# First stage of an adaLN linear-attention block: products of ones without a reader, products with silu(c) on repeated columns, another order of the first loads

## The chip, the core and the metric

The kernel runs on one core of a Trainium2 chip. The metric is the time of the device in microseconds, the median of several runs. The engines are TensorE (PE; PEld is its weight load), VectorE (DVE), ScalarE (ACT), GpSimd (POOL) and SyncE (SP), which issues most of the DMAs. All data are fp32; "fp32r" is the type in which most products run, with each operand split into a rounded part (hi) and the rest (lo).

## What is computed

`x` is 2048 x 576 (`S` x `D`), `c` is 1 x 576, `w_mod` is 576 x 3456.

```
mod = silu(c) @ w_mod                      # 6 rows of 576: sa, ca, ga, sb, cb, gb
h = layernorm(x) * (1 + ca) + sa
x = x + ga * linear_attention(h, wqkv, wo) # 32 heads of 18
h = layernorm(x) * (1 + cb) + sb
x = x + gb * (silu(h @ w1) @ w2)           # F = 4608
```

## The kernel before

The rows of x are worked on in 16 tiles of 128 rows, four to a block. Before any product of the attention can run, the kernel needs the first piece of `mod` (`sa` and `ca`) as columns, because it modulates the normalised, transposed x: chunk k of 128 features (five chunks, k = 0 to 4, the last with 64) gets `h = xT * scale + shift`, with scale and shift from `cols["a"]`, in the traces `col_a`.

The first stage, up to the products of the first two tiles with the weights of the keys, is written out by hand under `tc.manual_schedule()` (L374 to L454). Its order:

- `ident`, `ones`, `sel` and small constants are set; c is loaded as a row (`crow`), transposed on PE (L387) and turned into `sc = silu(c)`, one column per 128 features.
- Four tiles of x are loaded first (L259), then the pieces of `w_mod` of 128 rows and 2 x 576 columns into `mods[0]` to `mods[3]` (L265 to L269, `load_mod`), with the last 64 rows in `tmod` on ACT's queue, then `wqkv` in 15 pieces into the accumulators `acc` (keys, values, queries).
- `ln.stats`, `ln.finish` and `ln.normalise` are the layernorm of the four tiles: `bn_stats` on DVE, a power on POOL (L170), and the normalisation on DVE or ACT (L177, L179).
- The modulation is split. `mods[0]` and `mods[1]` go straight to PE (`mod_direct`, `mod_mm`, L329): the weights of the product are 128 columns of `w_mod`, the moving operand is one column of `sc`. `tmod` goes the same way with two columns, `sel`. `mods[2]` and `mods[3]` are scaled by `sc` and added on DVE (L340, L409) and their sum goes to PE with one column of `ones` (`col_mod`). All of these add up in PSUM, chunks 0 and 1 (`HEAD`) in one place, chunks 2 to 4 in another, so `col_a` is read in two steps (L348).
- `turn_tiles` transposes tiles 0 and 1 (L354). Chunk by chunk, `modulate` (L185, L187) and `split_h` (L191, L109) make hi and lo of h, `w_hi` (L282, on ACT) and `w_lo` (L287, L289, on POOL or DVE) make hi and lo of the weights, and `first_k` multiplies (`k_part`, L371). A second pass over the lo parts of the weights follows, one tile after the other.
- `k_phi` (L298 on ACT, `e`; L303 and L304 on DVE) applies phi to the keys.

What comes after, the values, tiles 2 and 3 (`turn_half`), the queries and the other blocks, is ordered on PE by the program and on the other engines by a planner with an estimate of times; a later part follows the lists in `ORDERS`.

Of the kernel before, what the change touches and what calls it, by code (L numbers as in the profile page):

```python
# [9 lines left out]
F32 = mybir.dt.float32  # L10
# [6 lines left out]
P = 128  # L17
# [5 lines left out]
def kernel(ctx: ExitStack, tc, A_x, A_wqkv, A_wo, B_x, B_w1, B_w2, c, w_mod, out):  # L23
# [28 lines left out]
    def f32(ap):  # L52
        return ap.bitcast(F32)
# [183 lines left out]
    def psT():  # L237
        t = psA.tile([P, 512], F32, name="psT")
        return t
# [16 lines left out]
    nc.scalar.dma_start(crow[0:KC, :], c[0, 0 : KC * P].rearrange("(j p) -> j p", p=P))  # L256
    nc.scalar.dma_start(crow[KC : KC + 1, :].rearrange("p (h r) -> p h r", h=2),
                        c[0:1, KC * P : D].unsqueeze(1).to_broadcast([1, 2, 64]))
    xts = x0s = [load_x(0, i) for i in range(4)]  # L259


    mod_room = hTa.tile([P, KC, 2, DX], F32, name="hT")
# [18 lines left out]
    def w_hi(wpart, k, full):  # L281
        return A.copy(wpart(k if k < KC else 2 * KC), full)  # L282
# [42 lines left out]
    def mod_mm(m, k, rhs, a=None, first=False, last=False):  # L325

        c = 2 * (k - HEAD if k >= HEAD else k)
        dst = mod_ps_a[k >= HEAD][:, c : c + 2] if a is None else mod_ps_a[k >= HEAD][:, c + a : c + a + 1]
        T.matmul(dst, m[:, k * P : (k + 1) * P], rhs, start=first, stop=last, skip_group_check=True)  # L329

    def mod_direct(m, rhs, first=False):
        A.copy(m[:, :, D:DX], m[:, :, KC * P : D])
# [4 lines left out]
    def add_mod(k0, k1):  # L337

        o = sums[:, :, k0 * P : min(k1 * P, D)]
        V.scalar_tensor_tensor(o, mods[3][:, :, k0 * P : min(k1 * P, D)], sc[:, 3:4], o, op0=ALU.mult, op1=ALU.add)  # L340
        if k1 > KC:
            V.tensor_copy(sums[:, :, D:DX], sums[:, :, KC * P : D])

    def col_mod(k0, k1):
        for k in range(k0, k1):
            for a in range(2):
                mod_mm(sums[:, a], k, ones[:, 0:1], a, last=True)
        V.tensor_add(cols["a"][:, k0:k1, :], mod_ps_a[k0 >= HEAD].rearrange("p (k a) -> p k a", a=2),  # L348
                     plus1.unsqueeze(1).to_broadcast([P, k1 - k0, 2]))

    def turn_tiles(pT, tiles, chunks):
# [15 lines left out]
    def k_part(tiles, passes, first=False, last=False):  # L367
        for n, (a, b) in enumerate(passes):
            for i in tiles:
                for h in range(2):  # L370
                    T.matmul(kps[i][:, h, :HALF], hT[0][:, a, i * P : i * P + P], wk_(b)[:, h * HALF : (h + 1) * HALF],  # L371
                             start=first and n == 0, stop=last and n == len(passes) - 1)

    with tc.manual_schedule():  # L374
        make_identity(nc, ident)
        V.memset(ones, 1.0)
        V.memset(sel, 0.0)
        V.memset(neghalf, -0.5)
        V.memset(eps, EPS)
# [7 lines left out]
        T.transpose(psc, crow, ident[: KC + 1, : KC + 1])  # L387
# [16 lines left out]
        pT = dict(enumerate((t[:, 0:256], t[:, 256:512], kvp[1][:, 0, :], kvp[1][:, 1, :], kvp[2][:, 0, :])))  # L404
# [8 lines left out]
        def first_k(k):  # L413
            k_part(range(2), [(k, k), (KC + k, k)], k == 0)
# [1065 lines left out]
```

## Time and profile before

| | |
|---|---|
| median of three runs | 1168.71 us (1167.72 to 1171.38) |
| span of the profiled execution | 1167.7 us; no other time of this execution is told |
| busy: PE, DVE, ACT, POOL | 1144.4, 977.4, 531.2, 660.1 us |
| first product with a piece of `w_mod` | 10.25 us |
| first and second `col_a` | 24.39 and 30.39 us |
| `e` of tile 0 (ACT L298) | 37.65 us |
| first product with `wq` | after 52.74 us |

The times in the table's lower half are from the timeline and from the chain of waits. In the profile, L12 is line 12 of the kernel. A row of the timeline has the start, the duration, the engine, the line, the operation, the tiles (out<-in), the shape, the count, and the idle time of the engine before it with what ended it. A product of fp32 (not fp32r) stands as two records of PE.

### The profile page before, as it was taken

Reading aid. Unit: us, or ns where it says so; the run is one execution under the profiler, and the core shown is the slowest. Engines: PE = TensorE matmul, PEld = TensorE weight load, DVE = VectorE, ACT = ScalarE, POOL = GpSimd, SP = SyncE. Lnnn points to the kernel's source line nnn. Section 1 sums busy time; section 2 is a strip of 40 time slices with the busy share of each in tenths; the row PEclk is TensorE's granted clock in tenths of the full one; section 3 lists DMA queues with packets and bytes.
Section 4 is the critical chain, followed back from the end, with each engine's and each line's share of the span. In section 5 each row is a group of like instructions: output and inputs, shape, how many; then the busy total and the mean of one; then the engine's idle time right before and its main releaser. Section 6 shows DMA issues by size and latency. Waiting matters only on the chain.

```text
span 1167.7 us, 19567 instructions
## 1 busy us (share of the span) xinstructions
PE 1144.4 (98%) x7203; PEld 1058.8 (91%) x7203; DVE 977.4 (84%) x1539; ACT 531.2 (45%) x1088; POOL 660.1 (57%) x749
## 2 busy tenths in 40 slices
PE   6899999999999999999999999999999999999998
PEld 6799999999998889999999999999999999999998
DVE  3857574478797899999999999999999999999996
ACT  3553433346556454444444454444444444444541
POOL 2500000164554387677677767757767776776686
PEclk9999999999999999999999999999999999999999
DMA  8303210022357879769769779688697697697684
GB/s 284 102 28 105 64 55 1 1 83 63 112 218 266 322 261 348 274 254 351 272 252 363 266 280 334 262 319 308 249 352 275 257 345 273 255 364 268 256 308 152
DMA packets 57231, 268.61 MB, mean 230 GB/s; under 512 B 5484, under 2 KB 19312, under 8 KB 34096
## 3 DMA queue, kind: packets, MB, share of 16 engines
q1 hardware_dynamic: 56964, 267.06, 62.2%
q8 instruction: 57, 0.93, 0.3%
q10 hardware_dynamic: 172, 0.30, 0.1%
q14 instruction: 38, 0.31, 0.1%
HBM read 250.56 MB, written 16.78 MB: 229 GB/s over the span
## 4 chain that ended last, share of the span: by engine, by line
PE 94%; DVE 2%; DMA 2%; ACT 1%; issue 0%; SPq 0%; DVEq 0%; ACTq 0%
PE up L1211 33%; PE down L1284 31%; PE psK L212 12%; PE big L212 7%; PE small L774 2%; PE big L785 2%; PE kvp L517 1%; PE kvp L329 1%; PE psK L668 1%; PE big L700 1%; DMA room<-hd 1%; DVE hT L109 1%; PE small L200 1%; DMA hT<-in_w_mod_dram 1%; PE up L1314 1%; PE down L1314 1%
## 5 line engine op out<-in xcount | busy, mean ns | idle before, releaser
L1292 DVE TENSOR_TENSOR acc<-down,acc 128x576 f32<-128x576 f32 x330 | 246.2, 754 | 14.1 <-PE down L1284 4.3
L1211 PE MATMUL up<-hT,w 128*128 128x512 f32 x916 | 240.3, 391 | 0.0
L1211 PEld LDWEIGHTS up<-hT,w 128*128 128x128 f32 x916 | 164.6, 188 | 25.8
L1246 POOL TENSOR_TENSOR s<-f,f 128x256 f32<-128x256 f32 x66 | 51.6, 782 | 163.9 <-ACT f L1227 163.9
L1284 PE MATMUL down<-w,hc 128*128 128x288 f32 x792 | 120.7, 294 | 0.0
L1284 PE MATMUL down<-w,hb 128*128 128x288 f32 x792 | 120.7, 294 | 0.0
L1284 PEld LDWEIGHTS down<-w,hb 128*128 128x128 f32 x792 | 113.5, 188 | 6.0 <-DVE U L1292 0.4
L1284 PEld LDWEIGHTS down<-w,hc 128*128 128x128 f32 x792 | 113.6, 188 | 5.6
L1292 DVE TENSOR_TENSOR U<-down,U 128x576 f32<-128x576 f32 x132 | 99.5, 754 | 18.0 <-PE down L1284 15.7
L109 DVE TENSOR_TENSOR w<-v,w 128x288 fp32r<-128x288 f32 (+1 forms) x170 | 111.8, 667 | 0.4 <-ACT w L954 0.4
L212 PE MATMUL psK<-w,hT 128*128 128x288 f32 (+2 forms) x660 | 108.0, 298 | 0.8 <-DVE w L287 0.6
L212 PEld LDWEIGHTS psK<-w,hT 128*128 128x128 f32 x660 | 95.0, 189 | 1.5 <-DVE w L287 0.8
L1211 PE MATMUL up<-room,w 128*128 128x512 f32 x348 | 93.2, 396 | 1.7 <-DMA room<-hd 1.7
L1265 POOL TENSOR_TENSOR hc<-s,hc 128x512 fp32r<-128x512 f32 x66 | 89.8, 1360 | 0.0
L1227 ACT ACTIVATE f<-f 128x512 f32<-128x512 f32 x102 | 64.4, 631 | 48.1 <-DVE f L1232 25.7
L1230 DVE TENSOR_TENSOR f<-up,p 128x512 f32<-128x512 f32 x102 | 69.7, 683 | 14.7 <-PE up L1211 10.1
L1211 PEld LDWEIGHTS up<-room,w 128*128 128x128 f32 x348 | 62.4, 188 | 13.0 <-DVE f L1232 2.1
L954 ACT CAST w<-v 128x288 fp32r<-128x288 f32 x85 | 36.5, 434 | 77.0 <-PE down L1284 52.1
L1250 POOL TENSOR_TENSOR f<-f,s 128x256 f32<-128x256 f32 x66 | 50.6, 767 | 34.4 <-DVE hb L1265 27.3
L1284 PE MATMUL down<-w,hd 128*128 128x288 f32 x396 | 63.2, 295 | 0.0
L1284 PE MATMUL down<-w,he 128*128 128x288 f32 x396 | 63.1, 295 | 0.0
L1284 PE MATMUL down<-w,ha 128*128 128x288 f32 x396 | 63.0, 294 | 0.0
(284 smaller groups left out, 2498.4 us busy)
## 6 DMA issues: line engine op xcount, KB each, us to landing
hT<-hd SPq DMA_DIRECT2D x66, 1280.0 KB, 5.8
hT<-hd SPq DMA_DIRECT2D x45, 1024.0 KB, 5.1
room<-hd SPq DMA_DIRECT2D x35, 1280.0 KB, 6.0
room<-hd SPq DMA_DIRECT2D x20, 1024.0 KB, 5.8
v<-in_B_w_dram SPq DMA_DIRECT2D x17, 576.0 KB, 7.3
v<-in_B_w_dram SPq DMA_DIRECT2D x17, 512.0 KB, 7.6
hd<-S SPq DMA_DIRECT2D x6, 1024.0 KB, 4.2
xt<-in_A_x_dram SPq DMA_DIRECT2D x16, 288.0 KB, 3.1
```

Source lines behind the costliest of these rows:

```text
L109: return V.tensor_sub(lo, full, f32(hi))
L212: T.matmul(ps, xpart(a), wpart(b), start=n == 0, stop=n == len(XW) - 1)
L774: T.matmul(ps, left, right, start=n == 0, stop=n == len(seq) - 1)
L954: A.copy(self.w2[n][:, 0], src)
L1211: T.matmul(ps, left, right, start=first and m == 0, stop=m == len(seq) - 1, skip_group_check=True)
L1227: A.activation(self.f[i, k], self.f[i, k], AF.Silu)
L1230: V.tensor_add(f, self.bank[bank[1]], self.p1)
L1246: G.tensor_add(self.s[:, 0:1], half(i, 0, 1), half(i, 1, 1))
L1250: G.tensor_sub(half(i, 1, 0), half(i, 1, 0), self.s[:, 1:2])
L1265: eng.tensor_sub(t[:, :, 1, :], src, f32(t[:, :, 0, :]))
L1284: T.matmul(ps[:, p, :HALF], self.a[i, n][:, u, p * P : (p + 1) * P], self.w.w2[n][:, v], start=n in (1, 5, 7, 6) and j == 0, stop=j == 2, ...
L1292: V.tensor_add(dst, ps[:, :, :HALF], dst)
```

## The change

Three things change, all in the first stage.

*Loads.* Tiles 2 and 3 of x are loaded behind the four pieces of `w_mod` instead of ahead of them. Their statistics, with a second `ln.finish`, move behind the sums of the modulation (tile 2) and the split of chunk 1 (tile 3), and their normalisation, on ACT, behind the casts of the key weights.

*Products with silu(c).* The moving operands get more columns: `scw` is 128 equal columns of `sc` (128 are used for chunks 0 and 1, 80 for chunks 2 to 4), `sel` is 48 columns twice, `ones` is used with 128 or 80 columns. The results lie in slots of 128 or 80 columns of two PSUM banks, of which one column is read. `scw` and `sel` are made on DVE in `z`, which is free until later; `mods[1]`'s products come ahead of the tail's and the transposes; the fifth transposed chunk gets another bank, and a copy of 64 columns moves from DVE to ACT.

*Products of ones.* `warm_up(8)` and `warm_up(10)` multiply `ones` with `ones` (128 columns) around the transpose of c; nothing reads the result.

```diff
-    xts = x0s = [load_x(0, i) for i in range(4)]
+    xts = x0s = [load_x(0, i) for i in range(2)]
...
     for k in range(1, KC):
         load_mod(mods[k], 0, k)
+    xts += [load_x(0, i) for i in range(2, 4)]
...
-    sel = pa.tile([P, 2], F32, name="sel")
+    WIDE, SLOTS = 48, (P, 80)
+    scw = z[:, : 2 * P].rearrange("p (j w) -> p j w", j=2)
+    sel = z[:, 2 * P : 2 * P + 2 * WIDE].rearrange("p (a w) -> p a w", a=2)
...
-    mod_ps_a = kvp[0][:, 0, 0 : 2 * HEAD], kvp[2][:, 1, 0 : 2 * (KC + 1 - HEAD)]
+    mod_bank = [kvp[j].rearrange("p a b -> p (a b)") for j in (0, 2)]
+    mod_slots = [b[:, : n * w].rearrange("p (k a w) -> p k a w", a=2, w=w)
+                 for b, n, w in zip(mod_bank, (2 * HEAD, 2 * (KC + 1 - HEAD)), SLOTS)]
+
+    def mod_mm(m, k, rhs, a, first=False, last=False):
+
+        slots, k0 = mod_slots[k >= HEAD], HEAD if k >= HEAD else 0
+        w = SLOTS[k >= HEAD]
+        dst = slots[:, k - k0, :, 0:WIDE] if a is None else slots[:, k - k0, a, :]
+        T.matmul(dst, m[:, k * P : (k + 1) * P], rhs if a is None else rhs[:, 0:w], start=first, stop=last, skip_group_check=True)
...
         if k1 > KC:
-            V.tensor_copy(sums[:, :, D:DX], sums[:, :, KC * P : D])
+            A.copy(sums[:, :, D:DX], sums[:, :, KC * P : D])
...
+    warm_ps = ps2()
+
+    def warm_up(n):
+        for _ in range(n):
+            T.matmul(warm_ps[:, 0, 0:P], ones, ones, start=True, stop=True)
...
+        warm_up(8)
         psc = psT()[:, : KC + 1]
         T.transpose(psc, crow, ident[: KC + 1, : KC + 1])
+        warm_up(10)
         A.activation(sc, psc, AF.Silu)
         A.activation(warm, sc[:, 0:1], AF.Exp)
         ln.stats(0, xts[0])
+        for j in range(2):
+            V.tensor_scalar(scw[:, j, :], ones, sc[:, j : j + 1], None, op0=ALU.mult)
         for a in range(2):
-            A.copy(sel[a * 64 : a * 64 + 64, a : a + 1], sc[a * 64 : a * 64 + 64, KC : KC + 1])
-        for i in range(1, 4):
-            ln.stats(i, xts[i])
-        ln.finish()
+            rows = slice(a * 64, a * 64 + 64)
+            V.tensor_scalar(sel[rows, a, :], ones[rows, 0:WIDE], sc[rows, KC : KC + 1], None, op0=ALU.mult)
+        ln.stats(1, xts[1])
+        ln.finish(0, 2)
 
-        mod_direct(mods[0], sc[:, 0:1], True)
+        mod_direct(mods[0], scw[:, 0, :], True)
         A.copy(tmod[:, D:DX], tmod[:, KC * P : D])
-        for k in START:
-            mod_mm(tmod, k, sel)
         ln.normalise(0, xts[0], xts[0], V)
         ln.normalise(1, xts[1], xts[1], A)
+        mod_direct(mods[1], scw[:, 1, :])
+        for k in START:
+            mod_mm(tmod, k, sel, None)
...
-        mod_direct(mods[1], sc[:, 1:2])
-        for i in (2, 3):
-            ln.normalise(i, xts[i], xts[i], A)
...
         add_mod(HEAD, KC + 1)
+        ln.stats(2, xts[2])
         first_k(0)
         col_mod(HEAD, KC + 1)
         turn_tiles(pT, (0, 1), (KC,))
         w_hi(wk_, 1, acc[1])
         split_h(*args[1])
+        ln.stats(3, xts[3])
+        ln.finish(2, 4)
         first_k(1)
...
         w_hi(wk_, 4, acc[4])
+        for i in (2, 3):
+            ln.normalise(i, xts[i], xts[i], A)
```

More of the change, by code (lines that the diff above doesn't have):

```diff
@@ L322 @@
     HEAD = 2
-    mod_ps_a = kvp[0][:, 0, 0 : 2 * HEAD], kvp[2][:, 1, 0 : 2 * (KC + 1 - HEAD)]
[L325 to L329, printed above, removed]
+    mod_bank = [kvp[j].rearrange("p a b -> p (a b)") for j in (0, 2)]
[6 more added lines that the diff above has]
+        T.matmul(dst, m[:, k * P : (k + 1) * P], rhs if a is None else rhs[:, 0:w], start=first, stop=last, skip_group_check=True)
     def mod_direct(m, rhs, first=False):
@@ L346, in col_mod @@
             for a in range(2):
-                mod_mm(sums[:, a], k, ones[:, 0:1], a, last=True)
-        V.tensor_add(cols["a"][:, k0:k1, :], mod_ps_a[k0 >= HEAD].rearrange("p (k a) -> p k a", a=2),
+                mod_mm(sums[:, a], k, ones, a, last=True)
+        V.tensor_add(cols["a"][:, k0:k1, :], mod_slots[k0 >= HEAD][:, :, :, 0],
                      plus1.unsqueeze(1).to_broadcast([P, k1 - k0, 2]))
@@ L372, in k_part @@
                              start=first and n == 0, stop=last and n == len(passes) - 1)
+    warm_ps = ps2()
+    def warm_up(n):
+        for _ in range(n):
+            T.matmul(warm_ps[:, 0, 0:P], ones, ones, start=True, stop=True)
     with tc.manual_schedule():
+        V.memset(ones, 1.0)
         make_identity(nc, ident)
-        V.memset(ones, 1.0)
         V.memset(sel, 0.0)
@@ L390 @@
         ln.stats(0, xts[0])
+        for j in range(2):
+            V.tensor_scalar(scw[:, j, :], ones, sc[:, j : j + 1], None, op0=ALU.mult)
         for a in range(2):
-            A.copy(sel[a * 64 : a * 64 + 64, a : a + 1], sc[a * 64 : a * 64 + 64, KC : KC + 1])
-        for i in range(1, 4):
-            ln.stats(i, xts[i])
-        ln.finish()
-        mod_direct(mods[0], sc[:, 0:1], True)
+            rows = slice(a * 64, a * 64 + 64)
[3 more added lines that the diff above has]
+        mod_direct(mods[0], scw[:, 0, :], True)
         A.copy(tmod[:, D:DX], tmod[:, KC * P : D])
-        for k in START:
-            mod_mm(tmod, k, sel)
         ln.normalise(0, xts[0], xts[0], V)
         ln.normalise(1, xts[1], xts[1], A)
+        mod_direct(mods[1], scw[:, 1, :])
+        for k in START:
+            mod_mm(tmod, k, sel, None)
         t = psT()
-        pT = dict(enumerate((t[:, 0:256], t[:, 256:512], kvp[1][:, 0, :], kvp[1][:, 1, :], kvp[2][:, 0, :])))
+        pT = dict(enumerate((t[:, 0:256], t[:, 256:512], kvp[1][:, 0, :], kvp[1][:, 1, :], kvp[0][:, 0, :])))
         turn_tiles(pT, (0, 1), range(KC))
-        mod_direct(mods[1], sc[:, 1:2])
-        for i in (2, 3):
-            ln.normalise(i, xts[i], xts[i], A)
         V.tensor_scalar(sums[:, :, 0:D], sums[:, :, 0:D], sc[:, 2:3], None, op0=ALU.mult)
```

## The prediction

> **What bounds the kernel now.** I read the page first, then the chain of waits up to 90 us, because the diff touches nothing later than that; then the timelines of the engines in that stretch.
>
> ```profile
> span 1167.7 us, 19567 instructions
> PE 94%; DVE 2%; DMA 2%; ACT 1%; issue 0%; SPq 0%; DVEq 0%; ACTq 0%
> ...
> 10.25 6.53 PE kvp L329 x30
> ...
> 18.59 5.78 PE kvp L329 x28
> ...
> 24.39 0.17 DVE col_a L348
> ...
> 28.77 1.59 PE kvp L329 x12
> 30.39 0.17 DVE col_a L348
> ...
> 37.65 0.66 ACT e L298
> ...
> 52.74 0.39 PE kvp L517
> 53.13 12.71 PE psK L212 x84
> ```
>
> The whole span is TensorE's, 94% of the chain. So what the first stage takes is added to a long run of products that waits for nothing, and an early gain is kept one for one if everything after it keeps its order. In the built programs it does: behind the first stage all five engines have the same instructions in the same order before and after.
>
> The chain to 24.39 us is almost only L329, the modulation's products. From 30.39 on it passes between DVE, ACT and POOL until the first product with `wq`, just after 52.74; from there it is PE again.
>
> Why are the L329 products slow? They have one column each, and two records per product (20 records for the ten products of a piece). The rows below are of the timeline, of single lines (least, median and longest ns), and of the table by stretches: its columns are the stretch, its length, the busy time and records of PE, PEld, DVE, ACT and POOL, the granted clock, the DMA share and GB/s. The last row is a group of the stretch 25.97 to 29.38.
>
> ```profile
> 22.51 1.84 PE L329 MATMUL kvp<-ones,hT 128*128 128x1 f32 x8
> L329 PE MATMUL kvp<-ones,hT x20: 205/352/353, 22.5 to 30.1; 128*128 128x1 f32 x20
> 115.72 1.06 PE L475 MATMUL psK<-ones,tmod 128*128 128x128 f32 x8
> L475 PE MATMUL psK<-ones,tmod x20: 274/275/377, 115.5 to 153.4; 128*128 128x128 f32 x20
> 114.15 1.21 PE L482 MATMUL psK<-tmod,ones 128*128 128x288 f32 x4 [0.17 <-DVE vx L109]
> 19.14:22.55 3.41, 3.41 (x18) 3.41 (x18) 0.00 (x0) 0.00 (x0) 0.00 (x0) 1.00 1.05 335
> 25.97:29.38 3.41, 3.41 (x17) 3.40 (x16) 2.17 (x3) 0.94 (x3) 1.42 (x1) 1.00 0.40 97
> 29.38:32.79 3.41, 3.04 (x23) 2.73 (x23) 1.66 (x5) 2.17 (x5) 0.55 (x1) 1.00 0.23 78
> 49.86:53.27 3.41, 1.34 (x9) 1.07 (x9) 3.41 (x8) 1.86 (x6) 1.99 (x2) 1.00 0.61 180
> 53.27:56.68 3.41, 3.41 (x16) 3.41 (x16) 3.41 (x14) 0.22 (x1) 0.00 (x0) 0.50 0.76 214
> L371 PE MATMUL psK<-w,hT 128*128 128x288 f32 x8 | 2.6, 482 | 1.3 <-ACT hT L191 1.3
> ```
>
> Early, one follows the other after (1.84 - 0.35) / 7 = 0.213 us; the same kind of product with 128 columns at 115.72 takes (1.06 - 0.275) / 7 = 0.112 us. So 128 columns cost nothing beside one, and the early ones run at half the clock. The granted clock reads 1.00 there, but the record has nothing before its first change; L329's pace changes at about 29.4 us, inside its last twelve. The row 53.27:56.68 is a recorded half clock (0.50): 16 records of 288 columns in 3.41 us, 0.21 each, where the chain from 53.13 on has 84 in 12.71, 0.15 on average, these among them.
>
> What raises the clock? In 19.14:22.55 PE is busy 3.41 of 3.41 us with one-column products and the clock stays low. In 25.97:29.38, before the rise, stand eight products of 288 columns (the last row): at the half clock's 0.21 us 1.7 us of streaming, half of the stretch. So columns count, not busy time. Products of fp32 stream more slowly: four of 288 columns at 114.15 take 0.3 us each at full clock, and by that 128 columns fill the whole 0.112 us. The added products are therefore denser than what raised the clock at 29.4.
>
> The Trainium skill (TensorE: Matmul & The Clock Gate, section "Why this matters for your kernels") asks for at least 4 us of continuous TensorE work to get the full clock. This trace disagrees with it as a rule on busy time: 14 us of back-to-back products from 10.25 on did not do it. By that rule alone the wide columns would add nothing, and the sum would be that of the first rival below.
>
> **The change part by part.**
>
> ```profile
> 4.91 0.24 PE L387 MATMUL psT<-ident,crow 5*128 5x5 f32 x1 [4.91 <-DMA crow<-in_c_dram]
> 10.25 4.40 PE L329 MATMUL kvp<-sc,hT 128*128 128x1 f32 x20 [5.11 <-DMA hT<-in_w_mod_dram]
> 5.00:10.00 5.00, 0.15 (x1) 0.06 (x1) 3.13 (x11) 1.93 (x5) 0.00 (x0) 1.00 1.05 332
> 14.74 0.75 DVE L340 SCALAR_TENSOR_TENSOR hT<-hT,sc 128x512 f32<-128x512 f32 x1 [0.69 <-DMA hT<-in_w_mod_dram]
> xt<-in_A_x_dram SPq DMA_DIRECT2D x16, 288.0 KB, 3.1
> 15.40 0.67 ACT L282 CAST w<-acc 128x576 fp32r<-128x576 f32 x1
> ```
>
> *Loads.* PE waits until 10.25 for the first piece of `w_mod`. Two tiles of x, 2 x 288 KB, no longer go ahead of it: at 332 GB/s that is 1.8 us, so about 8.4 us; the fourth piece comes at 12.9 instead of 14.7. The two tiles land behind it, and the weights of `wqkv` queue behind the same bytes as before, so the first cast (15.40) stays where it is.
>
> *Products of ones.* Eight products, 16 records at 0.213, take 3.4 us ahead of the transpose of c, which waits for its DMA until 4.91 anyway; ten more, 20 records, end at 9.4 us at half clock, or at about 7.5 if it rises meanwhile. They lie in idle time up to 8.4; the most that they can cost there is 1.0 us.
>
> *Wide products at full clock.* From 8.4: piece 0, 20 records x 0.112, to 10.6; piece 1 (there by then) to 12.9; the tail's 10 records to 14.0; eight transposes, which took 1.8 us at half clock (the chain, 16.78 to 18.59), to 14.9; the sum of pieces 2 and 3 is ready by 12.9 + 0.75; its eight records end at 15.8. `col_a` at 15.9 instead of 24.39: **-8.5**.
>
> ```profile
> 25.95 0.88 DVE L340 SCALAR_TENSOR_TENSOR hT<-hT,sc 128x640 f32<-128x640 f32 x1
> 26.86 1.31 DVE L342 COPY hT<-hT 128x128 f32<-128x128 f32 x1
> 12.55 0.28 ACT L332 COPY hT<-hT 128x128 f32<-128x128 f32 x1
> 30.47 0.41 DVE L109 TENSOR_TENSOR hT<-raw,hT 128x256 fp32r<-128x256 f32 x1
> 31.19 0.54 DVE L187 TENSOR_SCALAR raw<-kvp,col_a 128x256 f32<-128x256 f32 x1 [0.30 <-ACT raw L185]
> 33.88 0.53 DVE L187 TENSOR_SCALAR raw<-kvp,col_a 128x256 f32<-128x256 f32 x1
> 3.94 0.82 DVE L164 BATCH_NORM_STATS2 st<-xt 128x6 f32<-128x288 f32 x2 [2.83 <-DMA xt<-in_A_x_dram]
> 10.04 1.03 POOL L170 TENSOR_TENSOR rstd<-ve,neghalf 128x4 f32<-128x4 f32 x1 [5.87 <-DVE ve L169]
> 16.14 1.41 POOL L287 TENSOR_TENSOR v<-acc,w 128x576 fp32r<-128x576 f32 x1 [5.07 <-ACT w L282]
> 32.24 1.43 POOL L287 TENSOR_TENSOR w<-acc,w 128x576 fp32r<-128x576 f32 x1 [4.15 <-ACT w L282]
> 32.50 1.45 DVE L109 TENSOR_TENSOR hT<-raw,hT 128x256 fp32r<-128x256 f32 x1 [0.44 <-ACT hT L191]
> 12.74 2.57 ACT L177 ACTIVATE xt<-xt,nm,rstd 128x64 f32<-128x64 f32 x4
> 34.76 1.81 ACT L282 CAST w<-acc 128x576 fp32r<-128x576 f32 x3
> ```
>
> *To the second `col_a`.* It came 6.0 us after the first (24.39 to 30.39). Now: the second sum starts 1.56 us after the first `col_a` as before, 17.5, and ends at 18.35; the copy on ACT takes 0.28 instead of 1.31 on DVE; twelve records at 0.112 end at 19.8. Second `col_a` at 19.9, 4.0 us after the first: **-2.0**. The first of the moved statistics (some 1.0 us on DVE) lies beside these products and costs nothing; if those were short, it would cost up to 1.0.
>
> *The moved statistics.* Between the second `col_a` and the modulation of chunk 3 on DVE lay 0.8 us (30.39 to 31.19). Now DVE does there the split's subtraction, 0.4, the statistics of tile 3, 0.82 and their aggregation, 1.0 in all, waits for POOL's power, 1.03, and has two small operations, `ve` and `nm`, around it, some 0.2 each: 2.8 us, so +2.0. Queued behind `nm` on DVE are the modulations of chunks 3 and 4, for which ACT's casts and PE wait. POOL's queue has that power ahead of its three `w_lo`: the first, at 16.14 before, now starts at 22.7, and all three run to about 27.1. DVE's subtractions beside them are slow (32.50: 1.45 us beside the 1.43 us of POOL; 0.4 otherwise), two of them now instead of one. Modulation of chunk 4: 3.5 us after the second `col_a` before (33.88), 6.0 now. **+2.5**.
>
> *The moved normalisations.* Four ACT instructions, 2.57 us as at 12.74, stand between the cast of w_k(4) and the casts of w_v that precede `e`. Before, ACT had those three casts done at 36.57 and waited 1.1 us for PE. Now: chunk 4's cast from 26.5, w_k(4) to 27.4, normalisations to 29.9, two casts to 31.0. PE's transposes of tile 2, which the built order now has within the second pass, wait for the first half of the normalisations, 28.7; eight records behind them at 0.15 end tile 0's keys at 29.9, so ACT is the later. **+1.3**.
>
> Sum at `e`: -8.5 - 2.0 + 2.5 + 1.3 = -6.7, that is 31.0 instead of 37.65. From `e` to the first product with `wq` everything is as before, 15.1 us. Span 1167.7 - 6.7 = 1161.0. The timed runs go from 1167.72 to 1171.38, median 1168.71; the profiled span lies at their low end, 1.0 below the median, so I expect a median of **1162.0**.
>
> Bounds: the loads' share between 0 and 2.7 (ones end at 7.5 at the earliest); the fall of the clock at 53.27 costs half of 3.41, 1.7 us, which may go or come a second time; slow subtractions between 0 and 1.0 each, three more at most. For the likeliest case 1159.5 to 1164.5.
>
> **The rivals.** *The clock stays low as before* (ones or these operands don't count). Then the 50 records of the pieces go at 0.213 from 9.4 to 20.1, transposes to 21.9, the sums' eight to 23.6: `col_a` gains only 0.8, the second `col_a` about as much, and the moved work costs its 2.5 + 1.3 in full: +3.0, 1171.7; with one more fall of the clock, 1173.4, slower. It decides from less than 3.8 us gained at the second `col_a`. For it: no product of ones ahead of 29 us is in the trace. Against: the density above. 0.12.
>
> *The clock falls back between 13 and 33 us.* The trace kept it with 23 records in 29.38:32.79 and dropped it after nine in 49.86:53.27, so the limit lies between; the wait for the second pass, 27 to 29 us, makes such a stretch. One or two falls at 1.7 us: 1163.7 to 1165.4. The Trainium skill (same page, same section) has the clock fall only after idle gaps of about 3 us. Here it fell after 1.34 us of work in 3.41; by the page this rival could hardly occur. I give the row more weight: 0.18.
>
> *The pieces of `w_mod` come no earlier*, because the queue is shared anyway. PE then starts at 10.25: 1163.9. Against: x's tiles are ahead of them on one queue. 0.08.
>
> **How the numbers follow.** The likeliest case has 0.62. A measurement of this kernel tells about 0.3%, 3.5 us, from no change: below 1165.2 is faster. Faster: 0.62, most of the second rival, 0.14, and 0.07 of the third, 0.83. Slower (above 1172.2): half of the first rival, 0.06, and 0.01 for what I don't see. Same: 0.10. The range, 1158.5 to 1167.0, holds the likeliest case, the second and the third rival, and the fall at 53.27 gone.
>
> **What would show it.** PE's records of the wide products 0.11 us apart from 9 us on; `col_a` near 16 and 20; a DVE wait of 1 us for POOL's power near 22; POOL's first `w_lo` near 23; ACT's `e` near 31, right behind casts and not after a wait for PE; the first product with `wq` near 46. Records 0.21 apart at 12 us would make the first rival true; `e` below 29 would mean that the moved work costs less than I have it.

## The result and the profile after

The changed kernel takes 1167.07 us (median of 20 runs, 1164.63 to 1168.99), the kernel before 1169.04 beside it; the ratio is 0.9977 with a 95% interval of 0.9968 to 0.9985. So it is faster, by 2.0 us, where 6.7 were forecast; by the prediction's own line (faster is below 1165.2) it is no change, to which it gave 0.10. The profiled execution has a span of 1162.9 us and a time of 1164.63, the fastest of the twenty; every run's time is 1.7 to 1.85 us above its span.

The chain of waits of the kernel after (start, us, what):

```profile
1.72 8.10 DMA hT<-in_w_mod_dram
9.84 6.89 DMA acc<-in_A_wqkv_dram
...
24.14 1.35 DVE nm L171
...
48.94 0.39 PE kvp L536
49.32 11.18 PE psK L212 x84
```

PE's products are gone from the front of the chain: up to 24 us it is now loads, and then DVE. The first product with `wq` follows 48.94 instead of 52.74, and the 84 products take 11.18 us instead of 12.71, because no fall of the clock lies in them this time. The timelines of PE, DVE, POOL and ACT in the first stage:

```profile
7.79 0.61 PE L384 MATMUL psK<-ones 128*128 128x128 f32 x4
9.96 4.66 PE L335 MATMUL kvp<-z,hT 128*128 128x128 f32 x40 [1.56 <-DMA hT<-in_w_mod_dram]
...
27.17 1.17 PE L377 MATMUL psK<-w,hT 128*128 128x288 f32 x4 [2.90 <-DVE hT L109]
...
24.14 1.35 DVE L171 SCALAR_TENSOR_TENSOR nm<-mv,rstd 128x2 f32<-128x2 f32 x1 [0.82 <-POOL rstd L170]
25.41 0.53 DVE L187 TENSOR_SCALAR raw<-kvp,col_a 128x256 f32<-128x256 f32 x1
25.87 2.80 DVE L109 TENSOR_TENSOR hT<-raw,hT 128x256 fp32r<-128x256 f32 x2
...
23.40 0.71 POOL L170 TENSOR_TENSOR rstd<-ve,neghalf 128x2 f32<-128x2 f32 x1 [15.05 <-DMA acc<-in_A_wqkv_dram]
24.07 1.41 POOL L288 TENSOR_TENSOR v<-acc,w 128x576 fp32r<-128x576 f32 x1
25.42 2.96 POOL L288 TENSOR_TENSOR w<-acc,w 128x576 fp32r<-128x576 f32 x2
...
30.04 2.57 ACT L177 ACTIVATE xt<-xt,nm,rstd 128x64 f32<-128x64 f32 x4
32.52 1.23 ACT L283 CAST w<-acc 128x576 fp32r<-128x576 f32 x2
33.66 0.64 ACT L299 ACTIVATE e<-psK 128x576 f32<-128x576 f32 x1
```

Forty records of wide products take 4.66 us, (4.66 - 0.28) / 39 = 0.112 each: full clock. Behind 23.5 us DVE is the slow one: an `nm` of two columns takes 1.35 us, two subtractions 2.80, each beside a `w_lo` on POOL, and PE stands still for 2.90 us ahead of chunk 2. The table by stretches (stretch, length, busy time and records of PE, PEld, DVE, ACT and POOL, granted clock, DMA share, GB/s) shows what that pause does to the clock:

```profile
20.55:23.96 3.41, 2.92 (x23) 2.61 (x23) 1.98 (x8) 2.20 (x5) 0.56 (x1) 1.00 1.04 285
23.96:27.37 3.41, 0.51 (x4) 0.28 (x3) 3.23 (x4) 0.98 (x2) 3.41 (x4) 1.00 1.06 294
27.37:30.79 3.42, 3.42 (x16) 3.42 (x15) 2.92 (x5) 1.60 (x4) 1.02 (x1) 0.50 0.92 252
```

PE is busy for 0.51 of 3.41 us, and the next stretch has half the clock.

The milestones of all profiles of this case, read from the timelines (us; one execution each; "c2" is the second `col_a`, "wq" the first product with `wq`; the mean clock is that of all timed runs of the kernel):

| kernel | first wide product | first `col_a` | c2 | `e` | c2 to `e` | wq | span | median | mean clock |
|---|---|---|---|---|---|---|---|---|---|
| before | 10.25 | 24.39 | 30.39 | 37.65 | 7.26 | 52.97 | 1167.7 | 1169.0 | 0.9988 |
| after | 9.96 | 17.56 | 21.65 | 33.66 | 12.01 | 49.16 | 1162.9 | 1167.1 | 0.9964 |
| after_again | 8.83 | 16.42 | 20.51 | 32.95 | 12.44 | 48.40 | 1167.4 | 1167.4 | 0.9958 |
| products_only | 10.87 | 18.47 | 22.79 | 30.05 | 7.26 | 45.34 | 1158.1 | 1163.2 | 0.9983 |
| loads_only | 9.65 | 23.79 | 29.70 | 41.73 | 12.03 | 57.23 | 1171.1 | 1173.4 | 0.9982 |
| late_ln | 10.38 | 17.97 | 22.07 | 34.07 | 12.00 | 49.59 | 1164.5 | 1166.8 | 0.9958 |
| norm_late | 10.58 | 23.07 | 27.16 | 35.72 | 8.56 | 51.21 | 1164.4 | 1166.1 | 0.9970 |
| no_ones | 9.64 | 23.01 | 27.10 | 39.27 | 12.17 | 54.60 | 1168.5 | 1168.2 | 0.9968 |
| wide_no_ones | 10.25 | 21.57 | 25.89 | 33.16 | 7.27 | 48.45 | 1162.3 | 1163.7 | 0.9990 |
| narrow | 10.14 | 22.92 | 29.68 | 37.42 | 7.74 | 52.80 | 1167.3 | 1169.5 | 0.9893 |
| after_fill | 9.39 | 16.98 | 21.07 | 33.11 | 12.04 | 48.60 | 1162.3 | 1165.6 | 0.9983 |
| lo_first | 8.68 | 16.27 | 20.59 | 31.74 | 11.15 | 47.05 | 1161.8 | 1167.3 | 0.9946 |
| ln_gap | 9.54 | 17.14 | 21.58 | 31.00 | 9.42 | 46.51 | 1161.7 | 1164.3 | 0.9970 |
| products_again | 10.32 | 17.91 | 22.24 | 29.50 | 7.26 | 44.80 | 1158.3 | 1163.5 | 0.9978 |
| products_fill | 10.49 | 18.09 | 22.42 | 29.69 | 7.27 | 44.97 | 1161.2 | 1160.4 | 0.9994 |
| products_bridge | 10.25 | 17.84 | 22.16 | 29.42 | 7.26 | 44.72 | 1158.6 | 1160.35 | 1.0000 |

One stretch of 3.41 us at half clock lowers the mean over 1165 us by 0.0015, so 0.9964 is 2.4 such stretches in a run, 0.9988 is 0.8. The stretch ahead of the first rise is not in the mean: the 29 us of the kernel before alone would give 0.987.

### The profile page after: what moved, and what is told of

The parts are those of the page before. It is cut to its first block, busy times and chain, and to the rows that moved or that the text cites. A ratio compares the mean times of both kernels' runs of the same rounds, so it can differ in the third digit from the quotient of the medians.

```text
span 1162.9 us, 19645 instructions
## 1 busy us (share of the span) xinstructions
PE 1143.3 (98%) x7239; PEld 1056.8 (91%) x7239; DVE 979.1 (84%) x1544; ACT 531.6 (46%) x1087; POOL 661.8 (57%) x750
## 4 chain that ended last, share of the span: by engine, by line
PE 92%; DMA 4%; DVE 2%; ACT 1%; issue 0%; SPq 0%; POOL 0%; ACTq 0%; DVEq 0%; POOLq 0%
PE up L1230 33%; PE down L1303 31%; PE psK L212 12%; PE big L212 7%; PE small L793 2%; PE big L804 2%; PE kvp L536 1%; DMA acc<-in_A_wqkv_dram 1%; DVE hT L109 1%; PE psK L687 1%; DMA room<-hd 1%; PE big L719 1%; DMA hT<-hd 1%; DMA hT<-in_w_mod_dram 1%; PE small L200 1%; PE up L1333 1%
## 5 line engine op out<-in xcount | busy, mean ns | idle before, releaser
L170 POOL TENSOR_TENSOR rstd<-ve,neghalf 128x4 f32<-128x4 f32 (+3 forms) x10 | 9.6, 958 | 95.4 <-DVE ve L169 79.3
```

## The experiments

**Which half brings it, which half takes it back.** products_only keeps the ones and the wide products and undoes the moves:

```diff
-    xts = x0s = [load_x(0, i) for i in range(2)]
+    xts = x0s = [load_x(0, i) for i in range(4)]
...
-    xts += [load_x(0, i) for i in range(2, 4)]
...
-        ln.stats(1, xts[1])
-        ln.finish(0, 2)
+        for i in range(1, 4):
+            ln.stats(i, xts[i])
+        ln.finish()
```

with the normalisations of tiles 2 and 3 back behind the first transposes. loads_only is the reverse: the kernel before with these moves alone.

> The new kernel with the products of ones, the wide products and the copy on ACT, but with all four tiles of x loaded ahead of w_mod and the layernorm of tiles 2 and 3 where the kernel before has it. Theory A (the moved loads and the moved layernorm take back what the faster products bring: in the new kernel the first piece of w_mod landed at 9.85 us, only 0.3 earlier than before, w_qkv's pieces 1.4 us later, and chunk 4's modulation came 6.9 us after the second col_a instead of 3.5): first piece at 10.2, first col_a at 17.9, second at 22.0, chunk 4's modulation about 26.0, e at 30 (33.7 in the new kernel, 37.65 before), median about 3 us under the new kernel's: 1163.5 to 1164.5. Rival B (the falls of the clock in the K and V passes and behind them decide, and what comes earlier there is lost to another fall): e at 30 as well, but one more stretch of half clock between 20 and 60 us, and a median within 1 us of the new kernel's 1167.1. Rival C (w_qkv's pieces bind whatever stands ahead of them): e at 32 or later, median 1166 to 1167.

> The kernel before with only the moves: tiles 2 and 3 of x loaded behind w_mod, their statistics and normalisations at the new places; products one column wide, none of ones. Theory A: the pieces of w_mod at 9.9, PE at half clock up to about 29 us, col_a about 24.1 and 29.8, chunk 4's modulation 5 to 7 us after the second col_a, so 35 to 37 instead of 33.9, e at 40 to 41.5 instead of 37.65, median 2 to 4 us above the kernel before: 1171 to 1173. Rival B: the moved work lies beside the slow products and the waits for weights, e within 1 us of 37.65 and the median within 1 us of the kernel before.

products_only: 1163.2 us, ratio 0.9946 (0.9932 to 0.9959) to before. loads_only: 1173.4, ratio 1.0039 (1.0026 to 1.0052). The products bring 6 us, the moves cost 4 (a little more than the 2 to 4 expected), and the change is their sum. In products_only c2 to `e` is 7.26 us, to the hundredth that of the kernel before, and PE's pause ahead of chunk 2 is gone. Theory A holds. B falls, since the median is 3.9 us under the new kernel's, and C (w_qkv's pieces), since `e` comes at 30.05.

**Which of the moves.** late_ln has x's four tiles first and only the layernorm late; norm_late has the statistics early too, so that only the four normalisations on ACT are late:

```diff
 # late_ln, against the new kernel
-    xts = x0s = [load_x(0, i) for i in range(2)]
+    xts = x0s = [load_x(0, i) for i in range(4)]
...
 # norm_late, against products_only: the same two lines, moved
+        w_hi(wk_, 4, acc[4])
+        for i in (2, 3):
+            ln.normalise(i, xts[i], xts[i], A)
```

> The new kernel with all four tiles of x loaded ahead of w_mod, as in the kernel before, but with the statistics and normalisations of tiles 2 and 3 at their new, late places. Theory (the late layernorm is the cost, and the load order by itself brings a little): w_mod and w_qkv land as in the run with all of the layernorm early (first col_a about 18.4, second 22.7), chunk 4's modulation 6.5 to 7 us after the second col_a instead of 3.5, so at 29.4, e at 34 to 35, median about 4 us above that run's 1163.2: 1167 to 1168.5, no better than the new kernel. Rival (the later landing of w_qkv is the cost): with w_qkv early again e comes at 30 to 31 although the layernorm is late, median 1163 to 1164.5.

> x's four tiles loaded first and all statistics early, as in the kernel before, with the ones and the wide products; only the normalisations of tiles 2 and 3 stand late on ACT, ahead of the casts of w_v, as in the new kernel. It splits the 3.6 us between the run with all of the layernorm early (1163.2) and the one with all of it late (1166.8). If the normalisations cost the 1.3 us that they were given, or up to their whole 2.57: e at 31.3 to 32.6 instead of 30.05, median 1164.5 to 1165.8, and the statistics with POOL's power have the rest. If ACT has room for them there: e at 30.1, median 1163.2, and the statistics have all.

late_ln: 1166.8 (ratio 0.9987, 0.9972 to 1.0002), the time of the new kernel, with the old order of the loads. So the late layernorm is the cost, and the load order by itself is worth nothing that these runs can tell. norm_late: 1166.1 (0.9964, 0.9951 to 0.9976); c2 to `e` 8.56, 1.30 more than 7.26. ACT's timeline in norm_late:

```profile
32.11 2.57 ACT L177 ACTIVATE xt<-xt,nm,rstd 128x64 f32<-128x64 f32 x4
34.58 1.23 ACT L282 CAST w<-acc 128x576 fp32r<-128x576 f32 x2
35.72 0.64 ACT L298 ACTIVATE e<-psK 128x576 f32<-128x576 f32 x1
```

`e` comes right behind casts and normalisations, where the kernel before had 1.08 us to wait for PE. The statistics with POOL's power have the other 12.01 - 8.56 = 3.45 us. The medians do not split so cleanly (from 1163.2, 2.9 us of 3.6 for the normalisations): norm_late's runs lie in two groups, 1161.7 to 1163.6 and 1165.0 to 1168.1, and its profile has a fall of the clock at a place where, of the kernels with wide products, no other profile has one:

```profile
8.15:11.56 3.41, 0.98 (x9) 1.01 (x10) 1.85 (x8) 0.44 (x2) 1.04 (x1) 1.00 1.04 370
11.56:21.80 10.24, 10.24 (x51) 10.24 (x50) 2.37 (x4) 2.17 (x4) 1.40 (x1) 0.50 1.05 346
```

Between the last of the ones and the first wide product (10.58) a stretch was nearly empty, and the wide products ran at half clock up to 21.80; so `e` came at 35.72 and not at the 31.3 to 32.6 expected.

**Ones and columns.** no_ones is the new kernel without its 18 products of ones; wide_no_ones is products_only without them; narrow is products_only with operands one column wide, the ones kept:

```diff
 # no_ones, wide_no_ones
-        warm_up(8)
-        warm_up(10)
...
 # narrow
-    WIDE, SLOTS = 48, (P, 80)
+    WIDE, SLOTS = 1, (1, 1)
...
-        mod_direct(mods[0], scw[:, 0, :], True)
+        mod_direct(mods[0], sc[:, 0:1], True)
```

> The new kernel without its 18 products of ones. If the wide products raise the clock by themselves, they run at 0.213 us a record from 9.9 to about 13.7 and at 0.112 from there: first col_a about 19.9 instead of 17.6, second about 24.0, e about 2 us later than 33.7 or less (w_qkv's pieces, due at 16.7 to 31, hide part of it), median 1167 to 1169.5. If products of this width don't raise it (rival), the clock stays low up to about 25 us as in the kernel before, col_a at 23.5, median 1171 to 1173.

> x's four tiles and the layernorm as in the kernel before, wide products, no products of ones. The wide products start at 10.9 at 0.21 us a record and raise the clock at the end of the first window that they fill, 14 to 18 us (in the new kernel without ones it rose only at 21.7): first col_a 20.5 to 23 instead of 18.5, e at 32 to 34, median 1165 to 1168. Rival (the ones bring nothing once the loads bind): e within 0.7 us of 30.05 and the median within 1 us of 1163.2.

> x's four tiles and the layernorm as in the kernel before, with the products of ones, but the products with silu(c) and of the ones in the two modulations one column wide. If the clock goes by the columns that stream: it rises at 7 to 9 us with the products of ones and falls at the next window's end without them, 10 to 13.7, so that most of the 50 records of the pieces run at 0.21 us: first col_a 21 to 23 instead of 18.5, e at 32 to 34 instead of 30.05, median 1165 to 1168. If it goes by the share of time in which PE has anything to do (the rival): no fall, first col_a about 18.4, median as with wide products, 1163.2.

no_ones: 1168.2 (0.9988, 0.9975 to 1.0002), as expected, but not as expected on the way: the wide products raised the clock only at 21.71, so the first `col_a` came at 23.01 instead of 19.9. wide_no_ones: 1163.7 (0.9944, 0.9924 to 0.9963), the same as with the ones: the rival was right on the time. Its reason was wrong, since `e` came at 33.16 and not at 30.05. The ones bring 3.1 us at `e` in the profiles (30.05 against 33.16; 5.6 in the new kernel, 33.66 against 39.27) and only 0.5 to 1.1 in the medians, which is not clear of the spread of the runs. The stretches of norm_late, above, show one way in which a run can lose that gain; whether it is what the timed runs do isn't shown. narrow: 1169.5 (1.0003, 0.9991 to 1.0016): without the columns nothing is left, where 1165 to 1168 had been expected. Its table by stretches:

```profile
8.21:11.63 3.42, 1.49 (x14) 1.52 (x14) 2.10 (x9) 0.89 (x4) 1.04 (x1) 1.00 1.05 392
11.63:15.04 3.41, 3.41 (x18) 3.41 (x18) 1.55 (x3) 3.34 (x6) 0.00 (x0) 0.50 1.06 391
```

The ones had raised the clock, and it fell at 11.63, behind a stretch with 1.49 of 3.42 us busy. One-column products, which fill PE for 3.41 of 3.41 us, did not bring it back before 35.5. In norm_late it fell at the same place, 11.56, and the wide products had it back at 21.80; that pair shows what the columns do. It is no single execution: the clock of narrow's twelve runs is 0.987 to 0.991.

**The falls.** after_again is the new kernel a second time; after_fill adds products of ones, without a reader, to PE's pause:

```diff
         first_k(1)
+        fill = kvp[2][:, 0, 0:P]
+        for _ in range(12):
+            T.matmul(fill, ones, ones, start=True, stop=True, skip_group_check=True)
         modulate(*args[2], A)
```

> The new kernel unchanged, for a second profile and beside the others on the same chip. Expected: median 1166.5 to 1167.5; e at 33.7 as in the first profile; if this profile's time is nearer to the median than the first one's 1164.6 was, its clock shows one to three more stretches of 3.41 us at half speed, and the work behind the first stage is later by their cost.

> The new kernel with 12 more products of ones without a reader, between the first pass over chunk 1 and that over chunk 2, where PE stood still from 24.0 to 27.2 us. They last about 2.7 us at full clock and end ahead of the operand that chunk 2 waits for, so they delay nothing and only change the clock. If the fall at 27.4 us costs what its slow records lost (14 records at 0.24 instead of 0.13, 1.5 us, of which ACT's late casts hide a part): e at 32.2 to 33 instead of 33.7, median 0.7 to 1.7 us under the new kernel's 1167.1. If that fall is hidden behind the normalisations on ACT: e at 33.6, the median within 0.5 us.

after_again: 1167.4 (0.9984, 0.9970 to 0.9998), this time with a profile of 1167.4 us:

```profile
23.88:27.30 3.42, 1.27 (x8) 1.09 (x8) 3.42 (x4) 0.98 (x2) 3.37 (x3) 1.00 1.05 317
27.30:34.12 6.82, 6.16 (x25) 5.76 (x25) 4.45 (x8) 5.70 (x11) 0.00 (x0) 0.50 0.78 222
44.36:47.78 3.42, 1.53 (x8) 1.12 (x8) 3.42 (x7) 2.60 (x8) 2.77 (x2) 1.00 0.54 173
47.78:51.19 3.41, 3.17 (x13) 3.17 (x14) 3.41 (x14) 0.22 (x1) 0.00 (x0) 0.50 0.64 181
```

`e` is even earlier than in the first profile, 32.95, but from the first product with `wq` to the end it takes 1119.0 us instead of 1113.8. Two falls, at 47.78 and at 402.76, are a part of these 5.3; another part is shown below. after_fill: 1165.6 (0.9968, 0.9955 to 0.9981), mean clock 0.9983, no fall in its profile. But c2 to `e` is 12.04 as without the filling: a single fall at 27 us is hidden behind ACT's normalisations, as the second theory had it; with two in a row, in after_again, it is 12.44. Its median is 1.4 to 1.8 us below the two of the new kernel, but the intervals overlap, and where that lies no profile shows (the second theory allowed 0.5).

**DVE's wait.** lo_first computes POOL's `w_lo` of chunks 0 and 1 ahead of the power; ln_gap has, beside that, both statistics and the power in DVE's idle time ahead of the second `col_a`, and `nm` behind chunk 1's subtraction:

```diff
         w_hi(wk_, 0, acc[0])
+        w_lo(wk_, 0, acc[0], G)
...
         ln.stats(2, xts[2])
+        ln.stats(3, xts[3])       # ln_gap only, as the next line
+        ln.power(2, 4)
...
         w_hi(wk_, 1, acc[1])
+        w_lo(wk_, 1, acc[1], G)
         split_h(*args[1])
-        ln.stats(3, xts[3])       # ln_gap only, as the next two lines
-        ln.finish(2, 4)
+        ln.shift(2, 4)
```

> The new kernel with one order changed: POOL computes w_k's lower parts of chunks 0 and 1 as soon as their casts are there (about 17 and 21 us), ahead of the power of tiles 2 and 3, instead of three of them back to back behind that power. If the collision with them is what made DVE slow from 23.6 us on (nm 1.35 us instead of 0.16, the two subtractions 1.25 and 1.65 instead of 0.42): nm 0.2, subtractions mostly 0.4, chunk 4's modulation about 4.7 us after the second col_a instead of 7.0, PE's wait ahead of chunk 2 about 1 us shorter, e at 30.5 to 31.5 instead of 33.1 to 33.7, median 2 to 3 us under the new kernel's 1167.1. Rival (DVE is slow there for another reason, the weights' traffic say, or ACT binds e anyway): e within 0.7 us of 33.4, the median within 1 us.

> The new kernel with its load order and its late normalisations, but the statistics of both tiles and POOL's power in DVE's idle time ahead of the second col_a (19.9 to 21 us), the operation nm behind chunk 1's subtraction, and POOL's lower parts of w_k chunks 0 and 1 as soon as their casts are there: nothing then waits on DVE for POOL. Theory (the wait ahead of nm makes PE's pause of 2.9 us ahead of chunk 2, and that pause makes the falls of the clock): no pause over 1.5 us there, chunk 4's modulation 3.5 to 4.3 us after the second col_a (7.0 in the new kernel), e 8.6 to 9.5 us after it instead of 12.0, at 30 to 31, mean clock 0.998 instead of 0.996, median 1163 to 1165. Rival (the order of the loads, w_qkv 1.4 us later, makes that pause): pause of 2 us or more, clock 0.996, median 1166 to 1167.5.

DVE and PE of lo_first:

```profile
23.61 1.35 DVE L171 SCALAR_TENSOR_TENSOR nm<-mv,rstd 128x2 f32<-128x2 f32 x1 [0.83 <-POOL rstd L170]
24.88 0.53 DVE L187 TENSOR_SCALAR raw<-kvp,col_a 128x256 f32<-128x256 f32 x1
25.33 0.97 DVE L109 TENSOR_TENSOR hT<-raw,hT 128x256 fp32r<-128x256 f32 x2
...
25.80 1.33 PE L377 MATMUL psK<-w,hT 128*128 128x288 f32 x4 [2.59 <-DVE hT L109]
```

The two subtractions take 0.97 instead of 2.80, and c2 to `e` is 11.15 instead of 12.01. But the third `w_lo` still starts right behind the power, `nm` still takes 1.35 us, PE still pauses for 2.59, the clock falls for two stretches, and the median is 1167.3 (0.9987, 0.9973 to 1.0001). The table by stretches:

```profile
21.06:24.47 3.41, 1.80 (x10) 1.14 (x9) 2.51 (x6) 1.27 (x3) 1.88 (x3) 1.00 1.05 272
24.47:31.30 6.83, 5.50 (x23) 5.50 (x24) 4.46 (x9) 5.42 (x10) 0.47 (x1) 0.50 1.05 328
```

My expectation was wrong: taking away the slow subtractions alone buys nothing while the pause stays. ln_gap brings POOL's power and `nm` forward:

```profile
22.61 2.78 POOL L294 TENSOR_TENSOR w<-acc,w 128x576 fp32r<-128x576 f32 x2
22.68 1.37 DVE L173 SCALAR_TENSOR_TENSOR nm<-mv,rstd 128x2 f32<-128x2 f32 x1 [0.60 <-POOL rstd L170]
...
25.72 0.79 PE L383 MATMUL psK<-w,hT 128*128 128x288 f32 x4 [1.52 <-DVE hT L109]
```

```profile
24.27:27.68 3.41, 1.96 (x15) 1.96 (x15) 2.94 (x6) 2.17 (x5) 1.12 (x1) 1.00 1.05 323
```

(The second fence is of the table by stretches.) It takes 1164.3 us (0.9954, 0.9941 to 0.9968), 2.8 less than the new kernel, with the new order of the loads, the late normalisations, and a pause of 1.52 instead of 2.90 us; the clock kept its rate behind it. DVE still waits 0.60 us for the power, and `nm` is still slow beside a `w_lo`; "nothing waits" did not come true. But the power starts 0.17 us after c2 instead of 1.75, and `nm` ends 2.47 us after it instead of 3.84. So most of the pause came from where the power and `nm` stand, not from the later weights, which ln_gap keeps (and late_ln, with the weights early, has the same 2.90 us). The 1.52 are just over the theory's bound, and its mean clock (0.998) does not hold (0.9970).

**A version that beats both.** products_again is products_only once more. products_fill adds eight products of ones to two waits of the first products with `pk`, products_bridge, beside these, eight more at the start:

```diff
         for j in range(NHC):
+            if t == 0 and j in (2, 4):
+                for _ in range(j + 1):
+                    T.matmul(kvp[2][:, 1, 0:P], ones, ones, start=True, stop=True, skip_group_check=True)
...
 # products_bridge
-        warm_up(10)
+        warm_up(18)
```

> The run with x and the layernorm as before, ones and wide products, once more: median 1162.5 to 1164, e at 29.5 to 31, and in this profile one or two falls of the clock, since the first profile's 1159.8 was the fastest of its runs.

> The kernel with x and the layernorm as before, ones and wide products, and eight more products of ones without a reader in the two waits of the first group of products with pk (42.0 to 43.4 and 43.9 to 45.1 us). They keep a window of the clock full in which in other runs it fell (47.8 us in a run of the new kernel, 48.8 and 53.3 in others). Theory (such falls, 1.7 us each, are what lies between the fastest and the usual run): no fall from 41 to 60 us, median 0.5 to 1.5 us under 1163.2. Rival (they delay the products behind them, or the falls lie elsewhere): median the same or up to 0.5 us later.

> The fastest so far (x and the layernorm as before, ones and wide products, eight products of ones among the first with pk) with 8 more products of ones at the start, which end near 9.1 us instead of 7.3, so that fewer windows between the ones and the first wide product (10.3 us) stay empty; in one run such a window let the clock fall at 11.6. Theory: mean clock as good or better (1.0), median 1159.5 to 1161 against 1160.4. Rival (they delay the first wide product where the clock rises late): median 0.5 to 1 us later.

products_again: 1163.5 (0.9947, 0.9931 to 0.9963); its profile had no fall, against my expectation. products_fill: 1160.4 (0.9926, 0.9912 to 0.9939), 2.8 under products_only where 0.5 to 1.5 were expected. products_bridge: 1160.35 (0.9923, 0.9911 to 0.9936), with a mean clock of 1.000 in each of its five runs, 1159.2 to 1161.2 us. The two profiles without the fills had no fall either, so what speaks for the fills is the runs: a mean clock of 0.9983 and 0.9978 without them, 0.9994 and 1.0000 with them, and medians lower by about 3 us. Two stretches of products_bridge, the first ahead of the wide products, the second around the first products with `pk`, show where they lie:

```profile
7.36:10.25 2.89, 2.89 (x28) 2.89 (x27) 2.21 (x7) 0.12 (x1) 0.28 (x1) 1.00 1.04 370
29.42:44.72 15.30, 13.95 (x100) 12.86 (x99) 15.01 (x17) 12.23 (x27) 12.17 (x7) 1.00 0.26 87
```

(100 records between `e` and the first product with `wq`, where products_only had 84.) This is 8.6 to 8.9 us less than the kernel before and 6.7 less than the changed one. The falls that remain lie elsewhere: products_fill's profile has one at 146.15. One bridge more or less made no difference in the median.

## Why the prediction was wrong, step by step

The forecast was -6.7 us, the measured change -2.0. By the positions in the two profiles the miss of 4.7 lies so: 1.56 up to the first wide product, 0.2 from there to c2, 0.9 from c2 to `e` (33.66 instead of 31.0), 0.2 from `e` to the first product with `wq`, and 1.8 behind it. These are positions of one execution each, and they differ by some 0.7 us between two executions of the same kernel (49.16 and 48.40 at the first product with `wq`).

**Loads (-1.85): mis-sized.** The first wide product came at 9.96, not 8.4. The prediction took the pieces for one line, in which what stands ahead lands first. The table by stretches up to the first wide product shows why that is wrong, first after, then before:

```profile
0.00:9.96 9.96, 7.28 (x37) 6.88 (x38) 4.38 (x20) 3.06 (x5) 4.11 (x13) 1.00 0.81 250
```

```profile
0.00:10.25 10.25, 0.24 (x1) 0.21 (x2) 4.36 (x19) 3.33 (x7) 3.59 (x13) 1.00 0.81 246
```

By then 2.5 MB have moved in either kernel (250 GB/s in 9.96 us, 246 in 10.25), though 0.59 MB less stand ahead of the first piece in the new one. So other pieces move beside the first and share the rate, and bytes taken from ahead of it don't bring it forward one for one. Over all profiles the new order has the first wide product at 9.4 (seven, 8.68 to 9.96), the old at 10.4 (nine, 10.14 to 10.87): 1.0 us, not 1.85. This is the rival "the pieces come no earlier" by half. Nor did `wqkv` stay where it was: in the chain its first piece is issued at 9.84, where the first piece of `w_mod` has landed, and lands at 16.7 (cast at 15.40 before). late_ln and ln_gap show no cost of that which these runs could tell.

**Ones: right in the profile.** They end at 8.4 us and the clock is up from 6.89. In the timed runs they are worth nothing that can be told (wide_no_ones, products_only), and the gap behind them can drop the clock again (norm_late, narrow).

**Wide products, both sums (-8.6 from the first product to c2): right.** From the first product to the first `col_a` 7.60 us (forecast 7.5), to the second 4.09 more (4.0); the records go 0.112 apart. narrow beside norm_late confirms that it is the columns. The first rival, the clock as low as before, is out.

**Moved statistics (+2.5): +3.45.** The mechanism was right, the wait for POOL's power (0.82) and the `w_lo` behind it at 24.07 too; `nm` was put at 0.2 and took 1.35, which covers the excess; the two subtractions took 2.80, about the 1.45 each that the prediction gave them. `nm` begins 0.07 us after the `w_lo` at 24.07 and ends with it, at 25.5. The Trainium skill (SBUF — State Buffer, section "SBUF: two separate sides") says that a DVE operation with two SBUF inputs and a GpSimd operation that reads SBUF exclude each other for a whole instruction, whichever comes later blocking. The rows agree: `nm` with two inputs waits the 1.41 us of the `w_lo` out, while the modulation at 25.41, with its tile from PSUM, takes its usual 0.53. ln_gap repeats it: `nm` begins 0.07 us after a `w_lo`, at 22.68, and takes 1.37. The prediction had the row of such a slow subtraction (32.50) and did not apply it to a two-column operation.

**Moved normalisations (+1.3): right.** norm_late has +1.30.

**From `e` on, everything as before: right in order** (15.50 us to the first product with `wq`, 15.32 before) **and wrong in the time behind it.**

**"An early gain is kept one for one": the step that failed in its mechanism.** The prediction saw behind the first stage a long run of products that waits for nothing. But of the 3.8 us that the new kernel is ahead at the first product with `wq`, the medians keep 2.0, and of products_only's 7.6 they keep 6.0. The clock takes a part of it. The second rival named the place, the wait for the second pass, and the sign; it was put at 0.18, and came in five of the six profiles that have the late statistics without a filling or ln_gap's order (at 27.37 here, at 24.47 to 31.95 in the others; in the sixth, loads_only, the stretch with the pause had 1.89 us busy and kept the clock). Its price was wrong at that place, since one such stretch is hidden behind ACT; but a run of the new kernel has 2.4 falls where the kernel before has 0.8. With the stretches filled the gain is kept: products_fill and products_bridge are 8.0 and 8.2 us ahead at the first product with `wq`, and 8.9 and 8.6 in the medians. Falls are not the whole of it, though: of the new kernel's twenty runs the five at a clock of 0.999 take 1164.6 to 1167.6 us, the five at 0.994 take 1166.5 to 1168.6, which is 1.0 us on average for more than three falls.

Nor does that run of products wait for nothing. Laid product by product over the first profile, after_again loses 1.2 us up to 57 us, with the fall at 47.78, 2.3 from 386 to 407 us, with the fall at 402.76, and 2.5 between 147 and 152 us, where no fall lies. The rows there, first of after_again, then of the first profile:

```profile
144.67 1.42 DVE L487 SCALAR_TENSOR_TENSOR tmod<-raw,sc,tmod 128x1152 f32<-128x1152 f32 x1 [3.73 <-DMA raw<-in_w_mod_dram]
148.80 1.38 PE L494 MATMUL psK<-ones,tmod 128*128 128x128 f32 x10 [1.07 <-DVE a L304]
151.50 1.24 PE L501 MATMUL psK<-tmod,ones 128*128 128x288 f32 x4 [1.32 <-DVE col_b L496]
```

```profile
141.70 1.42 DVE L487 SCALAR_TENSOR_TENSOR tmod<-raw,sc,tmod 128x1152 f32<-128x1152 f32 x1 [1.32 <-DMA raw<-in_w_mod_dram]
148.54 1.24 PE L501 MATMUL psK<-tmod,ones 128*128 128x288 f32 x4 [0.26 <-DVE col_b L496]
```

DVE can start on the last pieces of `w_mod` for the second modulation (`raw`) only 7.3 us behind their issue (at 137.39) instead of 4.9 (at 136.83), and PE waits for DVE. The kernel is the same, so this is the spread of a load: 4.2 to 7.3 us in the sixteen profiles, 5.7 in that of the kernel before, where PE waits 1.07 us for the last of these products. It can hide or feign a gain of this size in a single profile, but no run shows that it costs the new kernel more than the old. So of the 1.8 us that are lost behind the first stage a part is the clock; how large a part, and why the later falls are more frequent than in the kernel before, is not settled.

Beside the falls the Trainium skill (TensorE: Matmul & The Clock Gate, section "Why this matters for your kernels") warns of gaps of about 3 us. The pause of 2.90 us would fit that. wide_no_ones does not: its clock fell at 48.78, and the longest pause in the stretch before is 1.10 us.

```profile
46.53 0.74 PE L529 MATMUL kvp<-pk,vx 128*128 128x256 f32 x4 [1.10 <-DVE vx L109]
```

```profile
45.36:48.78 3.42, 1.35 (x9) 1.09 (x9) 3.42 (x8) 1.86 (x6) 1.98 (x2) 1.00 0.59 178
```

The measurement decides: it is the busy share of the stretch, 1.35 of 3.42 us, and not one long gap.

**From the span to the median (+1.0): 0.7 short.** The prediction set the span 1167.7 beside the times of the runs; every run's time is about 1.7 us above its own span. This moves the 1162.0, not the change of 6.7.

## What to carry to other kernels

When a change pulls work forward by clearing the way for it, price what is pushed into its place: here the faster products brought 6 us and the layernorm moved behind them cost 4 of these; ln_gap won 2.8 back by placing GpSimd's power, and the tiny operation that waits for it in DVE's queue, earlier. A faster stage also has more clock to lose: look for every wait of PE that leaves a stretch of 3.4 us less than about half busy, and put products without a reader into it; then look at the runs, for products_fill gained by it and after_fill's gain is not clear of the noise. And don't read a gain off one profile, where a kernel's falls of the clock and the landing of a load come and go from run to run; compare positions in the trace first, then medians and mean clocks.

## What the runs showed of the hardware

- Over all sixteen profiles, in stretches of 3.41 us counted from a recorded change of the clock: each of the 16 falls between 1 and 1150 us (PE's ends are modelled) followed a stretch in which PE was busy for 1.80 us or less (0.51 to 1.80). Stretches of 1.57 to 1.80 went either way, no stretch below 1.57 kept the clock, and none of 1.82 or more lost it (ln_gap's 1.96 above kept it).
- Each rise followed a stretch with 2.87 us busy or more, but busy time does not suffice: narrow's products of one column fill their stretches and raise nothing. Wide products raise it alone, after two full stretches at 18.06 in wide_no_ones, and after three at 21.71 in no_ones and at 21.80 in norm_late; why two or three is open.
- Where the stretches lie differs from run to run (the first rise of the kernels with ones is anywhere from 3.99 to 9.17 us), so the same pause costs a fall in one execution and none in the next: the waits shortly before the first product with `wq` have one behind them at 47.78 in after_again and none in the first profile of the same kernel.
